# Later landing times in a planner's list of steps: an attention and MLP kernel whose order is computed at build time

## The chip, the cores and the metric

The kernel runs on one core of one Trainium2 chip. The metric is the device time of one execution in microseconds (us). Before the change it is 307.97 us, the median of three runs (307.48 to 308.44).

## The reference

Clustered attention, then an MLP. For 4 batches, 8 heads, 768 rows and 64 dimensions per head:

```
mask   = argmax(q_n . c_n) == argmax(k_n . c_n)      # 16 centroids per head, normalised rows
scores = where(mask, q k^T / sqrt(64), -1e9)
attn   = softmax(scores) ; o = attn v
x      = o as [3072 rows, 512]
h      = x @ w_in [512, 2048] ; g = h * sigmoid(h) ; out = g @ w_out [2048, 512]
```

Every row of q and k is assigned to one of 16 clusters; only pairs in the same cluster attend to each other.

## The kernel before, in words

**Parts.** The rows of q and k of a pair of heads come in by DMA (`nk`, `nq`, `nv`). A *part* prepares some of them: a scaled f16 copy `hi` (L527 to L531) and the remainder `lo` (the split, DVE, L535) go to `hl`; the rows are transposed into `ab`, in batch 0 on TensorE (L570), in batches 1 to 3 by a DMA transpose on SP's queue (`turn_dma`, L550). In batches 1 to 3 there are 24 parts, one for each batch and head, each of 12 tiles of 128x128 (6 of k, 6 of q).

**Codes.** The mask is computed inside the score matmul. On the transposed rows TensorE makes the *logits* against the centroids (L624, 12 matmuls). DVE reduces them (L641) and takes the maximum (L661), POOL subtracts it (L673), DVE marks the assigned cluster (the one-hot rows `oh`, L700 and L702) and turns them in blocks of 32 (the flip, `ohT`, L715). Four *code copies* then put `ohT` into 16 more rows of `ab` (`put`): three on POOL (L732), one as a 12 KB DMA on SP (L728). A score matmul (L801) contracts over these 80 rows, so that pairs of different clusters get a large negative score.

**Attention.** Per head 9 units of up to 512 columns: scores (L801) into a PSUM bank, exponential on ACT (L808) into `P`, then the product with v (L829, with a column for the sum), and DVE normalises (L842, L847) into `xn`. A pair of heads is turned into `xt`, by a DMA transpose on SP (`turn_x`, L866) or by TensorE (L877) and a copy on DVE or ACT (L884).

**MLP.** Batch 0 has three units of 256 rows, batches 1 to 3 two of 384 rows each. Per unit 16 *up* steps (L907, four matmuls), tanh on ACT (L913) into `tn`, the gate on DVE (L918) into `gq`, then the *down* matmuls (L942), a copy out (L955, L957) and the store (L960). The weights come in twelve pieces by POOL's DMA queue (`weight`, L974 to L980), each started after some exponential.

**What sets the order.** The program creates all steps with an engine, an estimated duration, a priority (`key`) and what they depend on. `Plan.order()` then plays them through once: at each turn it takes the step that can start first by its estimates (then the one with the lowest key), and the resulting list is emitted. Each engine executes its instructions in that order, and waits where an operand isn't there. The plan's clock is used for nothing else: it holds no time on the chip. A step's estimated end decides when its readers count as ready, and so what is put ahead of them:

```
complete(s, t + s.w + s.lag)                                   # a step on an engine
tail = self.TURNED if s.flip else self.EARLY if s.start < 2000 else self.LAND
complete(s, stop + tail + s.slack)                             # a transfer, stop: its bytes are through
```

`TURNED` is 1000 ns, `LAND` 1250. A transposing transfer enters the model's queue 300 ns after its issue, with a load of 195 ns for each tile. Buffers rotate in pools (`hl` 3, `ab` 5, `ohT` 3, `tn` 3, PSUM 8 banks), and a step takes the buffer that comes free first by the plan. TensorE also gets matmuls on zeros (L353) in gaps of the plan early on.

Of the kernel before, what the change touches and what calls it, by code (L numbers as in the profile page):

```python
# [198 lines left out]
def kernel(  # L199
# [84 lines left out]
    step = plan.step  # L284
# [17 lines left out]
    COLD = 8500.0  # L302
    MORE = 250.0
    LATE = 600
    AT = [32.0, 63.0, 104.0, 133.9, 193.2, 273.6]
    ML = [55.5, 127.6, 75.5, 138.3, 182.4, 254.3, 222.5, 316.0, 335.3, 350.3]
    PUTB = ["POOL", "POOL", "SP", "POOL"]
# [166 lines left out]
    def part(b, p, segs, a0, due, lead=20.0, hi_eng="POOL", turn="DMA", twin=False, sub="POOL", code_eng=None, pace=None, wait=None):  # L474

        key = due - lead
        span = lead / 20.0
        n = sum(j1 - j0 for _, _, j0, j1 in segs)
        if (b, p) not in abuf:
            abuf[b, p] = buf("ab")  # L480
        A = abuf[b, p]
        hl = buf("hl")
        nk, nq = nks.get((b, p)), nqs.get((b, p))
        his, los = [], []
# [18 lines left out]
        for kind, h, j0, j1, t, hs in merged:  # L503
# [35 lines left out]
            w = {"ACT": act_w(64 * m), "DVE": dve_w(64 * m, 0.55), "POOL": pool_w(64 * m)}[hi_eng]  # L539
            x = step(hi_eng, w, hi, after=lds, use=[nat, hl], key=key, pace=pace)  # L540
# [5 lines left out]
        if turn == "DMA":  # L546

            def turn_dma():
                src = T["hl"][hl.i][:, 0 : n * pitch]
                nc.sync.dma_start_transpose(T["ab"][A.i][:, a0 : a0 + n, :], src)  # L550

            turned = [step("SP", 120 * n, turn_dma, after=[his, los], use=[hl, A], key=key + 2 * span, load=195 * n, flip=True, slack=LATE)]
        else:

            Z = buf("lt")
            chunks, where = [], {}
            for hh in sorted({h for _, h, _, _, _ in runs}):
                c = [t + i for _, h, j0, j1, t in runs if h == hh for i in range(j1 - j0)]
                if chunks and len(chunks[-1]) + len(c) <= 8:
                    chunks[-1] += c  # L560
                else:
                    chunks.append(c)
            for t in sum(chunks, []):
                where[t] = len(where)

            def turn_of(c, bank, c0, c1):
                def turn_pe():
                    pt = banks[bank.i].bitcast(f16)
                    for i, t in enumerate(c):
                        nc.tensor.transpose(  # L570
                            pt[0 : c1 - c0, i * 128 : (i + 1) * 128], tiles_of(hl)[:, t, c0:c1], ident
                        )

                return turn_pe

            def settle_of(c, bank, rows_, dst, eng):
                def settle():
                    pt = banks[bank.i].bitcast(f16)[0:rows_, 0 : len(c) * 128]
                    out_ = dst()[0:rows_, where[c[0]] : where[c[0]] + len(c), :].rearrange("p n c -> p (n c)")
                    if rows_ < 128 and eng == "ACT":  # L580
                        nc.scalar.activation(out=out_, in_=pt, func=AF.Copy, bias=0.0, scale=gain[0:rows_])
                    elif rows_ < 128:
                        nc.vector.tensor_scalar(out=out_, in0=pt, scalar1=gain[0:rows_], scalar2=None, op0=ALU.mult)  # L583
                    elif eng == "ACT":
                        nc.scalar.copy(out_, pt)
                    else:
                        nc.vector.tensor_copy(out_, pt)

                return settle

            def settle_w(c, eng):
                return act_w(128 * len(c)) + 60 if eng == "ACT" else dve_w(128 * len(c), 0.55, 40)

            turned = []
            for c in chunks:
                bank = buf("M")
                x = step("PE", 57 * len(c), turn_of(c, bank, 0, 128), after=[s_ident, his, los], use=[hl, bank], key=key + 2 * span)
                turned.append(
                    step(
                        turn[0], settle_w(c, turn[0]), settle_of(c, bank, 128, lambda: T["lt"][Z.i], turn[0]),  # L600
                        after=[x], use=[bank, Z], key=key + 3 * span,
                    )
                )
# [109 lines left out]
        if turn == "DMA":  # L713
            def flip():
                nc.vector.transpose(  # L715
                    T["ohT"][ohT.i][:, 0:n, :].rearrange("p n c -> p (n c)"),
                    T["oh"][oh.i][:, 0:n, :].rearrange("p n c -> p (n c)"),
                )

            s_flip = step("DVE", dve_w(32 * n, 1.04, 95), flip, after=marks, use=[oh, ohT], key=key + 12 * span)  # L720
            placed = []
            for g in range(4):

                def put(g=g):
                    dst = T["ab"][A.i][64 : 64 + HC, a0 : a0 + n, 32 * g : 32 * g + 32]
                    src = T["ohT"][ohT.i][32 * g : 32 * g + HC, 0:n, :]
                    if code_eng[g] == "SP":
                        nc.sync.dma_start(dst, src)  # L728
                    elif code_eng[g] == "ACT":
                        nc.scalar.copy(dst, src)  # L730
                    elif code_eng[g] == "POOL":
                        nc.gpsimd.tensor_copy(dst, src)  # L732
                    else:
                        nc.vector.tensor_copy(dst, src)

                w = {"ACT": 200 + act_w(32 * n) * 0.75, "POOL": pool_w(32 * n), "DVE": dve_w(32 * n, 0.08, 240), "SP": 600}[code_eng[g]]
                load = 10 * n if code_eng[g] == "SP" else None
                placed.append(step(code_eng[g], w, put, after=[s_flip, s_log], use=[ohT, A], key=key + 13 * span, load=load, port=code_eng[g] == "DVE"))

        else:  # L740
            last = {}
            for c in chunks:
                bank = buf("M")
                x = step("PE", 57 * len(c), turn_of(c, bank, D, HW), after=[marks, his, s_ident], use=[hl, bank], key=key + 12 * span)
                x = step(
                    turn[1], settle_w(c, turn[1]),
                    settle_of(c, bank, HW - D, lambda: T["ab"][A.i][:, a0 : a0 + n, :], turn[1]),
                    after=[x], use=[bank, A], key=key + 13 * span,
                )
                for t in c:  # L750
                    last[t] = x
# [10 lines left out]
    def attention(b, h, j0, j1, key, per, turn):  # L762

        p = h // 2
        A = abuf[b, p]
        nq = j1 - j0
# [91 lines left out]
        done = xn_done[b, p, j0]  # L858
# [4 lines left out]
        if turn == "DMA":  # L863

            def turn_x():
                nc.sync.dma_start_transpose(  # L866
                    T["xt"][X.i][:, p, cols].rearrange("p (n c) -> p n c", c=128),
                    T["xn"][xn.i][:, 0:nq, :].rearrange("p n c -> p (n c)"),
                )

            x = step("SP", 1240, turn_x, after=done, use=[xn, X], key=key + per - 3, load=195 * nq, flip=True, slack=LATE)
        else:
            bank = buf("M")

            def turn_x():
                for n in range(nq):
                    nc.tensor.transpose(banks[bank.i].bitcast(f16)[:, 128 * n : 128 * n + 128], T["xn"][xn.i][:, n, :], ident)  # L877

            def settle_x():
                dst, src = T["xt"][X.i][:, p, cols], banks[bank.i].bitcast(f16)[:, 0 : 128 * nq]  # L880
                if turn == "ACT":
                    nc.scalar.copy(dst, src)
                else:
                    nc.vector.tensor_copy(dst, src)  # L884

            x = step("PE", 57 * nq, turn_x, after=done, use=[xn, bank], key=key + per - 3)
            w = act_w(128 * nq) if turn == "ACT" else dve_w(128 * nq, 0.55, 40)
            x = step(turn, w, settle_x, after=[x], use=[bank, X], key=key + per - 3)
# [80 lines left out]
    def weight(kind, n, event):  # L969

        x, use, name = event

        def f():
            nc.gpsimd.tensor_copy(pace, T[name][use.i][:, D : D + 1])  # L974
            if kind == "in":
                nc.gpsimd.dma_start(
                    win_s[:, :, ts(n, 512)], moe_w_in.rearrange("(r p) f -> p r f", p=128)[:, :, ts(n, 512)]
                )
            else:
                nc.gpsimd.dma_start(  # L980
                    wout_s[:, 2 * n : 2 * n + 2, :],
                    moe_w_out[256 * n : 256 * n + 256, :].rearrange("(c p) d -> p c d", p=128),
                )

        return step("POOL", 840, f, after=[x], use=[use], key=-1, load=2450 if kind == "in" else 1220)


    want = {(n, h): AT[n] + (AT[n + 1] - AT[n]) * h / H for n in range(NU + B - 1) for h in range(H)}
# [104 lines left out]
```

## Time and profile before

| | |
|---|---|
| median of the runs | 307.97 us (307.48 to 308.44) |
| the profiled execution | 307.14 us, of it span 305.3 us |
| TensorE clock granted (mean) | 0.998 |
| exponentials L808 on ACT | 157.8 us busy, x288 |
| scores L801 on TensorE | 90.9 us, x384 |
| up L907, down L942 on TensorE | 95.6 us x576, 97.1 us x400 |
| DMA, share of the 16 engines from 51 to 205 us | 0.80 |
| DMA, the same from 205 us to the end | 0.13 |

How to read it: busy time is the sum of the records of an engine; on TensorE (PE) the records of successive matmuls overlap, and their ends are modelled. A row of the timeline has the start in us, the length in us, the engine, the line, the operation with output<-inputs, and in brackets the idle time before it with what ended it. SPq is SP's DMA queue: a row there is the time in which SP issued a transfer, not its flight.

### The profile page before, as it was taken

Reading aid. Unit: us, or ns where it says so; the run is one execution under the profiler, and the core shown is the slowest. Engines: PE = TensorE matmul, PEld = TensorE weight load, DVE = VectorE, ACT = ScalarE, POOL = GpSimd, SP = SyncE. Lnnn points to the kernel's source line nnn. Section 1 sums busy time; section 2 is a strip of 40 time slices with the busy share of each in tenths; the row PEclk is TensorE's granted clock in tenths of the full one; section 3 lists DMA queues with packets and bytes.
Section 4 is the critical chain, followed back from the end, with each engine's and each line's share of the span. In section 5 each row is a group of like instructions: output and inputs, shape, how many; then the busy total and the mean of one; then the engine's idle time right before and its main releaser. Section 6 shows DMA issues by size and latency. Waiting matters only on the chain.

```text
span 305.3 us, 8425 instructions
## 1 busy us (share of the span) xinstructions
PE 297.3 (97%) x3257; PEld 196.1 (64%) x3257; DVE 207.9 (68%) x493; ACT 223.7 (73%) x461; POOL 108.2 (35%) x218
## 2 busy tenths in 40 slices
PE   8999999999999999999999998999999999999995
PEld 6898777577677746666656765665655565554644
DVE  5999688778869955989766997867562323750820
ACT  5869999888988838999777998778782380642721
POOL 2546432656466480717564563733000000000000
PEclk9999999999999999999999999999999999999999
DMA  7999969993969888486969848472010201002001
GB/s 245 290 249 251 206 104 224 103 248 87 226 100 237 191 167 196 138 156 162 237 149 223 155 154 169 131 129 66 0 37 36 84 12 71 35 0 73 32 34 69
DMA packets 73688, 41.82 MB, mean 137 GB/s; under 512 B 53041, under 2 KB 70705, under 8 KB 73649
## 3 DMA queue, kind: packets, MB, share of 16 engines
q1 hardware_dynamic: 68944, 36.94, 51.4%
q0 software_dynamic: 4288, 4.20, 8.6%
q8 instruction: 25, 0.41, 0.6%
q10 hardware_dynamic: 416, 0.16, 0.2%
q14 instruction: 15, 0.11, 0.1%
HBM read 27.30 MB, written 6.29 MB: 110 GB/s over the span
## 4 chain that ended last, share of the span: by engine, by line
PE 80%; DMA 7%; ACT 5%; DVE 3%; issue 1%; POOL 1%; SPq 0%; ACTq 0%; POOLq 0%
PE bank L942 27%; PE bank L907 22%; PE bank L801 16%; PE bank L829 9%; ACT P L808 4%; DMA ab<-hl 3%; PE bank L570 3%; DMA wout_s<-in_moe_w_out_dram 2%; PE bank L624 2%; DMA nk<-in_k_dram 2%; POOL hl L531 1%; PE bank L615 1%; DVE hl L535 1%; DVE gq L918 1%; PE bank L619 1%
## 5 line engine op out<-in xcount | busy, mean ns | idle before, releaser
L808 ACT ACTIVATE P<-bank 128x512 f16<-128x512 f32 x288 | 157.8, 640 | 30.8 <-PE bank L801 29.1
L942 PE MATMUL bank<-wout_s,gq 128*128 128x512 f16 (+1 forms) x400 | 97.1, 370 | 0.4 <-DMA wout_s<-in_moe_w_out_dram 0.4
L907 PE MATMUL bank<-xt,win_s 128*128 128x384 f16 (+1 forms) x576 | 95.6, 308 | 0.0
L918 DVE SCALAR_TENSOR_TENSOR gq<-tn,bank 128x384 f16<-128x384 f32 (+1 forms) x144 | 70.1, 504 | 32.4 <-ACT tn L913 28.7
L801 PE MATMUL bank<-ab 80*128 80x256 f16 (+1 forms) x384 | 90.9, 326 | 0.0
L913 ACT ACTIVATE tn<-bank 128x384 f32<-128x384 f32 (+1 forms) x144 | 67.8, 488 | 24.1 <-PE bank L907 20.9
L907 PEld LDWEIGHTS <-win_s 128*128 128x128 f16 x576 | 55.0, 97 | 28.8
L942 PEld LDWEIGHTS <-gq 128*128 128x128 f16 x400 | 37.9, 98 | 33.1 <-issue 0.7
L829 PEld LDWEIGHTS <-P 128*128 128x128 f16 x1152 | 45.6, 97 | 11.9 <-ACT P L808 0.8
L829 PE MATMUL bank<-vt,P 128*128 128x65 f16 x1152 | 49.8, 193 | 0.7 <-ACT P L808 0.6
L732 POOL COPY ab<-ohT 16x384 f16<-16x384 f16 x72 | 39.3, 546 | 28.2 <-DVE ohT L715 11.7
L801 PEld LDWEIGHTS <-ab 80*128 80x128 f16 x384 | 34.6, 97 | 20.7 <-DVE ab L583 0.2
L673 POOL TENSOR_TENSOR Df<-L,mx 128x192 f32<-128x192 f32 x24 | 12.3, 511 | 41.9 <-DVE mx L661 39.7
L957 DVE COPY ot<-bank 128x512 f32<-128x512 f32 x18 | 12.3, 681 | 16.4 <-PE bank L942 15.6
L535 DVE SCALAR_TENSOR_TENSOR hl<-nk,hl 128x384 f16<-128x384 f32 (+1 forms) x29 | 19.8, 687 | 3.3 <-POOL hl L531 3.1
L535 DVE SCALAR_TENSOR_TENSOR hl<-nq,hl 128x384 f16<-128x384 f32 (+3 forms) x33 | 20.9, 635 | 0.6 <-POOL hl L531 0.3
L641 DVE TENSOR_REDUCE L<-bank 128x192 f32<-128x384 f32 x24 | 13.3, 552 | 10.0 <-PE bank L624 9.7
L847 DVE TENSOR_TENSOR xn<-bank,rz 128x384 f16<-128x384 f32 (+2 forms) x40 | 19.1, 477 | 1.4 <-DVE rz L842 0.2
L531 POOL TENSOR_SCALAR hl<-nk 128x384 f16<-128x384 f32 (+1 forms) x25 | 13.6, 547 | 7.6 <-PE bank L570 6.7
L955 ACT COPY ot<-bank 128x512 f32<-128x512 f32 (+1 forms) x7 | 3.7, 524 | 17.2 <-PE bank L942 17.2
L531 POOL TENSOR_SCALAR hl<-nq 128x384 f16<-128x384 f32 (+2 forms) x27 | 15.2, 566 | 1.7 <-DMA nq<-in_q_dram 1.1
L417 POOL CAST vt<-nv 128x384 f16<-128x384 f32 x26 | 14.6, 582 | 1.1 <-DMA nv<-in_v_dram 0.7
(60 smaller groups left out, 183.6 us busy)
## 6 DMA issues: line engine op xcount, KB each, us to landing
nv<-in_v_dram SPq DMA_DIRECT2D x16, 384.0 KB, 5.6
out_dram<-ot SPq DMA_DIRECT2D x23, 256.0 KB, 2.3
nk<-in_k_dram SPq DMA_DIRECT2D x15, 384.0 KB, 4.3
nq<-in_q_dram SPq DMA_DIRECT2D x12, 384.0 KB, 4.7
wout_s<-in_moe_w_out_dram POOLq DMA_DIRECT2D x8, 256.0 KB, 7.2
win_s<-in_moe_w_in_dram POOLq DMA_DIRECT2D x4, 512.0 KB, 9.3
nq<-in_q_dram SPq DMA_DIRECT2D x4, 256.0 KB, 6.5
nk<-in_k_dram SPq DMA_DIRECT2D x2, 192.0 KB, 2.8
```

Source lines behind the costliest of these rows:

```text
L417: (nc.gpsimd if eng == "POOL" else nc.vector).tensor_copy(dst, src)
L531: nc.gpsimd.tensor_scalar(out=dh, in0=src, scalar1=qs, scalar2=1.0, op0=ALU.mult, op1=ALU.mult)
L535: nc.vector.scalar_tensor_tensor(out=dl, in0=src, scalar=qs, in1=dh, op0=ALU.mult, op1=ALU.subtract)
L732: nc.gpsimd.tensor_copy(dst, src)
L801: nc.tensor.matmul(banks[sb.i][:, at : at + 128 * (c1 - c0)], ab[0:80, kt[j], :], ab[0:80, qt + c0 : qt + c1, :].rearrange("p n c -> p (n ...
L808: nc.scalar.activation(out=T["P"][P.i][:, 0:at], in_=banks[sb.i][:, 0:at], func=AF.Exp, bias=0.0, scale=ESC if b else -ESC)
L829: nc.tensor.matmul(banks[O.i][:, (D + 1) * t : (D + 1) * t + nn], w, vt[:, VW * j : VW * j + nn], start=(j == 0), stop=(j == NJ - 1), skip ...
L847: nc.vector.tensor_tensor(out=T["xn"][xn.i][:, 0:nq, (h % 2) * D : (h % 2) * D + D], in0=banks[O.i][:, 0 : (D + 1) * nq].rearrange("p (t c ...
L907: nc.tensor.matmul(banks[bank.i][:, 0:n], win_s[:, r, ts(fb, 128)], T["xt"][xtb[b].i][:, r, 128 * j0 : 128 * j1], start=(r == 0), stop=(r ...
L913: nc.scalar.activation(out=T["tn"][tn.i][:, 0:n], in_=banks[bank.i][:, 0:n], func=AF.Tanh, bias=0.0, scale=1.0)
L918: nc.vector.scalar_tensor_tensor(out=T["gq"][g.i][:, fb % 4, 0:n], in0=T["tn"][tn.i][:, 0:n], scalar=1.0, in1=banks[bank.i][:, 0:n], op0=A ...
L942: nc.tensor.matmul(banks[bank.i][:, 0 : c1 - c0], T["gq"][gqs[fc // 4].i][:, fc % 4, ts(t, 128)], wout_s[:, fc, c0:c1], start=(fc == 0), s ...
```

## The change

Three allowances in the planner's model are changed. A transposing transfer (the parts of batches 1 to 3 and the `xn` of a pair of heads) counts as landed 1500 ns instead of 600 ns after the modelled end; the code copies of batches 1 to 3 on POOL count as done 600 ns later (on SP the argument has no effect, since a transfer's end doesn't use `lag`); a weight piece counts as landed 600 ns later. No instruction is added or removed, and no size changes: only the order of the list, and with it which of the rotating buffers and banks each step gets.

```diff
     LATE = 600
+    FLIP = 1500
+    DONE = 600
+    WSL = 600
...
-            turned = [step("SP", 120 * n, turn_dma, after=[his, los], use=[hl, A], key=key + 2 * span, load=195 * n, flip=True, slack=LATE)]
+            turned = [step("SP", 120 * n, turn_dma, after=[his, los], use=[hl, A], key=key + 2 * span, load=195 * n, flip=True, slack=FLIP)]
...
-                placed.append(step(code_eng[g], w, put, after=[s_flip, s_log], use=[ohT, A], key=key + 13 * span, load=load, port=code_eng[g] == "DVE"))
+                placed.append(step(code_eng[g], w, put, after=[s_flip, s_log], use=[ohT, A], key=key + 13 * span, load=load, port=code_eng[g] == "DVE", lag=Plan.LAG.get(code_eng[g], 0) + DONE))
...
-            x = step("SP", 1240, turn_x, after=done, use=[xn, X], key=key + per - 3, load=195 * nq, flip=True, slack=LATE)
+            x = step("SP", 1240, turn_x, after=done, use=[xn, X], key=key + per - 3, load=195 * nq, flip=True, slack=FLIP)
...
-        return step("POOL", 840, f, after=[x], use=[use], key=-1, load=2450 if kind == "in" else 1220)
+        return step("POOL", 840, f, after=[x], use=[use], key=-1, load=2450 if kind == "in" else 1220, slack=WSL)
```

In the list as built, TensorE's rows are the same up to the logits of the first part of batch 1 (51.6 us in the trace of before); POOL's and SP's lists differ from about there on too. From then to the last parts the logits of most parts stand behind more work than before, and some code transfers and transposes change places on SP. After the last part's logits TensorE's order is again nearly the same.

## The prediction

> **What bounds the kernel now.** The page comes first: the span, the share of TensorE (PE), and the chain that ended last.
>
> ```profile
> span 305.3 us, 8425 instructions
> PE 297.3 (97%) x3257; PEld 196.1 (64%) x3257; DVE 207.9 (68%) x493; ACT 223.7 (73%) x461; POOL 108.2 (35%) x218
> ...
> PE 80%; DMA 7%; ACT 5%; DVE 3%; issue 1%; POOL 1%; SPq 0%; ACTq 0%; POOLq 0%
> ```
>
> PE is the bound, and 80% of the chain is its own work. The change removes no instruction and adds none, so PE's 3257 matmuls stay; it can win or lose only in the time in which PE stands. How much is that? A matmul's record overlaps the next one's, so "97% busy" hides short stands. The tail of the kernel shows PE running without a break:
>
> ```profile
> 259.93 10.56 PE L907 MATMUL bank<-xt,win_s 128*128 128x384 f16 x64
> 270.33 10.52 PE L942 MATMUL bank<-wout_s,gq 128*128 128x512 f16 x48
> 280.69 10.56 PE L907 MATMUL bank<-xt,win_s 128*128 128x384 f16 x64
> ```
>
> The first group's record ends at 259.93 + 10.56 = 270.49, yet the next group starts at 270.33. So an unbroken PE starts its next matmul 0.16 us ahead of the end of the last record, and a stand is (start of a matmul − end of the record before it + 0.16). The spacings are 10.40 / 64 = 0.162 us for 384 columns and 10.36 / 48 = 0.216 us for 512. From these rows, too: from 260 us on nothing is left to win.
>
> Now the places where PE stands after 51 us (the two lists of steps are equal on PE up to there). The timeline of PE, five pairs of rows:
>
> ```profile
> 53.02 0.59 PE L801 MATMUL bank<-ab 80*128 80x512 f16 x2
> 54.00 0.38 PE L942 MATMUL bank<-wout_s,gq 128*128 128x512 f16 x1 [0.39 <-DMA wout_s<-in_moe_w_out_dram]
> ...
> 57.55 0.60 PE L942 MATMUL bank<-wout_s,gq 128*128 128x512 f16 x2
> 58.14 0.21 PE L624 MATMUL bank<-stk,ab 128*128 128x32 f16 x2
> ...
> 62.51 0.60 PE L801 MATMUL bank<-ab 80*128 80x512 f16 x3
> 63.24 0.21 PE L624 MATMUL bank<-stk,ab 128*128 128x32 f16 x2
> ...
> 136.04 0.65 PE L907 MATMUL bank<-xt,win_s 128*128 128x384 f16 x3
> 137.07 0.29 PE L624 MATMUL bank<-stk,ab 128*128 128x32 f16 x5 [0.38 <-DMA ab<-hl]
> ...
> 187.45 0.38 PE L801 MATMUL bank<-ab 80*128 80x512 f16 x1
> 188.77 0.47 PE L624 MATMUL bank<-stk,ab 128*128 128x32 f16 x12 [0.94 <-DMA ab<-hl]
> ```
>
> By that rule PE stands 0.55, 0.15, 0.29, 0.54 and 1.10 us. The first is for a weight piece (w_out). The other four all stand ahead of L624, the logits of a part, which read the transposed rows `ab` just moved by DMA: 2.08 us together. That is what this change can win, 0.7% of the time; shorter stands than 0.15 I leave out on both sides.
>
> **The change part by part.** I number the 24 parts of batches 1 to 3 by the order of their logits, 0 to 23, and give a step's place on PE as the sum of the spacings of all matmuls ahead of it. Places can be compared between the lists, because the durations are the same and PE hardly stands.
>
> *The transposing transfers (FLIP).* The planner took a 12-tile transfer to be usable 0.30 + 2.34 + 1.00 + 0.60 = 4.24 us after its issue; now 5.14.
>
> ```profile
> ab<-hl SPq DMA_TRANSPOSE x24, 4.1
> ab<-ohT SPq DMA_DIRECT2D x24, 12.0 KB, 2.8
> ```
>
> ```profile
> 183.53 3.60 SPq L550 DMA_TRANSPOSE ab<-hl  x2
> ```
>
> ```profile
> L550 SPq DMA_TRANSPOSE ab<-hl x24: 1294/1461/5414, 44.4 to 200.2; - x24
> ```
>
> The three fences are the DMA issues (last column: median us to landing), SP's timeline at part 20, and the transposes' rows on SP (min/median/max ns, while SP is held). Half the transfers land in 4.1 us or less, but PE waits for the slow half: part 20's was issued at 183.53 and its logits could start at 188.77, 5.24 later. A plan with 4.24 puts the logits 1 us early, and that is the 1.10 us stand. The Trainium skill's page "DMA: Bandwidth & Descriptors" speaks against the change here: its figures (a fixed cost of about 2.0 us, "Anatomy of one DMA", and 261 GB/s for a transpose, "Latency and other measured facts") give an estimate of 2.0 + 393 KB / 261 GB/s = 3.5 us for these 12 tiles. By that the old 4.24 would be ample and the time would stay at 307.97; the row of 4.1, and 5.24 where it matters, says otherwise, so the measurement decides.
>
> What each of the four stands becomes, by the places in the two lists:
> - Part 20 (1.10). Ahead of its logits the new list puts 6 attention matmuls (L829, 0.03 each, 0.18), a score (0.22) and two down matmuls (0.43): 0.82 us of work that stood right behind them. DVE's split rows ahead of the transfer keep their place, so it lands when it did: 1.10 − 0.82 = 0.28 stays.
> - Part 13 (0.54). Two 256-column scores (0.22) go ahead of the logits. On DVE a gate row moves behind the two splits that the transfer waits for:
>
> ```profile
> 130.02 0.54 DVE L918 SCALAR_TENSOR_TENSOR gq<-tn,bank 128x384 f16<-128x384 f32 x1
> 130.48 0.72 DVE L535 SCALAR_TENSOR_TENSOR hl<-nk,hl 128x384 f16<-128x384 f32 x1
> 131.12 0.55 DVE L535 SCALAR_TENSOR_TENSOR hl<-nq,hl 128x384 f16<-128x384 f32 x1
> ```
>
>   so the transfer can go 130.48 − 130.02 = 0.46 earlier. 0.22 + 0.46 exceeds 0.54: gone.
> - Part 1 (0.15). A score (0.22) and 18 attention matmuls (0.53) go ahead: gone.
> - Part 2 (0.29). Its logits come 0.96 earlier, but its transfer passes two entries of SP's queue (the first code transfer and a transpose of `xn`), which in the trace held SP from 55.57 to 58.18, and its splits pass part 0's one-hot rows on DVE. It is issued near 55 to 56 instead of 58.27. More than 0.96 is gained: gone.
>
> ```profile
> 55.57 1.02 SPq L728 DMA_DIRECT2D ab<-ohT  x1
> 56.97 1.21 SPq L866 DMA_TRANSPOSE xt<-xn  x1
> 58.27 4.34 SPq L550 DMA_TRANSPOSE ab<-hl  x2
> ```
>
> Together 2.08 − 0.28 = 1.80 won. The transposes of `xn` take the same allowance; the up matmuls that read them (unit 1 of the MLP) go from place 58.6 to 59.9.
>
> *The code copies (DONE).* POOL's copies count as done 0.60 later, so scores keep more room. From a part's logits to its first score the shortest room was 8.1 us (part 0) and is now 7.2 (part 1); part 0's chain in the trace ran from its logits to the landing of its code transfer:
>
> ```profile
> 51.63 0.45 PE L624 MATMUL bank<-stk,ab 128*128 128x32 f16 x12
> ```
>
> 55.57 + 2.8 − 51.63 = 6.7 us. It still fits by 0.5 us (part 1's own chain was longer only by the two transposes that held SP from 58.27 to 62.61 and now go sooner): cost nothing, and if that cover is gone, the overrun itself.
>
> *The weight pieces (WSL).* The last of the twelve goes in the unchanged part of POOL's list:
>
> ```profile
> 46.37 0.77 POOL L980 DMA_DIRECT2D wout_s<-in_moe_w_out_dram  x1
> ```
>
> The w_out piece with the 0.55 stand keeps its first reader at the same place (47.84): nothing won.
>
> *What is late next.* The new list puts part 3's logits (place 57.91) ahead of unit 1's up matmuls (59.95), and on DVE part 2's one-hot block and part 3's two reductions ahead of the `xt` copy for which those wait. Durations from this stretch:
>
> ```profile
> 63.81 0.56 DVE L641 TENSOR_REDUCE L<-bank 128x192 f32<-128x384 f32 x1 [0.39 <-PE bank L624]
> 64.41 0.35 DVE L661 TENSOR_REDUCE mx<-L 128x12 f32<-128x192 f32 x1
> 64.68 0.41 DVE L884 COPY xt<-bank 128x512 f16<-128x512 f16 x1
> 65.01 0.68 DVE L957 COPY ot<-bank 128x512 f32<-128x512 f32 x1
> 65.61 0.20 DVE L702 TENSOR_SCALAR oh<-Df 128x96 f16<-128x96 f32 x1
> 65.72 0.20 DVE L700 TENSOR_SCALAR oh<-Df 128x96 f16<-128x96 f32 x1
> 65.96 0.58 DVE L715 STREAM_TRANSPOSE ohT<-oh 128x384 f16<-128x384 f16 x1
> ```
>
> Part 2's logits at 55.56 let the reduction start 0.57 later (63.81 − 63.24), at 56.13. From a reduction's start to its one-hot rows the trace has 65.61 − 63.81 = 1.80, so 57.93, and the flip ends 0.93 on (65.96 + 0.58 − 65.61), at 58.86. Then the reduction (0.60 to the next row), the maximum (0.27) and the copy (0.41) end at 60.14; 0.2 for the release makes 60.35 against 59.95: a new stand of 0.40. Below, it could be 0, if one-hot rows come sooner; above, twice that, 0.8, if POOL's subtraction is late by as much again. I take 0.40, to which the rows lead.
>
> **Sum:** −2.08 + 0.28 + 0.40 = −1.40 us. Against the profiled execution (307.14 us, span 305.3 and 1.84 around it) that is 305.74; against the median of the runs shown, 307.97, it is 306.57. I take 306.6.
>
> **The rivals.** *Paid back.* The work put ahead of the logits must itself be ready. While PE stood 1.10 us, ACT and DVE caught up; without the stand, the score and the down matmuls put ahead of part 20 wait for a bank or a gate. And DVE now runs part 20 and 21's splits and part 19's one-hot rows ahead of a gate, some 0.64 + 0.11 + 0.24 + 0.58 = 1.6 us by the spacings above; the same happens at part 13. If PE pays most of one such block, about 1.0 us of the 1.40 are back: 307.6. For it: three `tn` buffers tie ACT to those gates. Against: up matmuls are about 1 us apart there, so three buffers cover 3 us.
>
> *Slower: SP's queue.* Part 0's code transfer now stands behind two transposes on SP. If these go at 55.0 and 56.5, SP is free near 58.0, and the code lands at 60.8. Its first score has place 56.83; part 1's logits have 51.78 and stood at 58.14, so with the 0.15 gone 6.2 are to be added, and it comes near 63.0. That is room of 2.2. But a transpose holds SP for 1.46 us in the middle and 5.41 at most (the row of L550; the longest stood behind two loads). If both take the longest, the code lands 7.9 later and PE stands 5.7; if one, 4.0 later and 1.8. It decides from 2.2 + 1.4 = 3.6 us of extra delay, where the stand eats the gain. Between 306.6 + 1.8 = 308.4 and 306.6 + 5.7 = 312.3; I take 309.4, near the lower end, since one long hold in 24 is what the trace shows. Against: no load is queued just ahead of them. The same order recurs at parts 17 and 19.
>
> *Nothing gained.* The transfers could slide by the same amount as their readers, if the splits wait for late PE work. For part 20 the list shows that they do not. The time would be 307.9.
>
> **How the numbers follow.** This kernel's measurement tells 0.3% (0.92 us) from no change, so faster is below 307.05 and slower above 308.89. Forecast 306.6: 0.52, its own range 305.6 to 307.0. The two cases in which it is paid back or not gained (307.6 to 307.9): 0.23. The queue (309.4): 0.25, which stands for other new waits of that size too, since the lists differ over 150 us. The range takes in the forecast with every stand gone and no new one (307.97 − 2.08 = 305.9, and about half of the 0.55 besides, 305.6), and the queue case up to its taken time: 305.6 to 309.4.
>
> **What would show it.** Right: no idle time of 0.3 us or more ahead of L624; at part 20 at most 0.3; PE's rows from 210 us on shifted by 1.4 us and otherwise equal; transfers still 4 to 5 us. Wrong: L801 waiting for `ab<-ohT` or POOL near 63 us; L907 waiting for the `xt` copy near 66 us by more than 0.8; L907 or L942 waiting for DVE's gates near 131 or 183 us; or logits that still wait because the transfers moved with them.

## The result, and the profile after

The changed kernel takes 305.12 us, the median of six runs (304.89 to 305.97), against 307.38 us for the kernel before on the same chip (six runs, 306.31 to 308.44). The ratio is 0.9929, with a 95% interval of 0.9905 to 0.9953: 0.7%, or 2.2 us, faster. The forecast was 306.6 us, and 305.12 lies 0.5 us below the range's low end of 305.6.

The page of the changed kernel (profiled execution: 305.97 us), the same three lines as in the prediction:

```profile
span 303.8 us, 8413 instructions
PE 297.6 (98%) x3257; PEld 196.6 (65%) x3257; DVE 206.6 (68%) x493; ACT 222.1 (73%) x461; POOL 110.2 (36%) x218
...
PE 82%; DMA 8%; ACT 3%; DVE 2%; POOL 2%; issue 1%; SPq 0%; POOLq 0%; ACTq 0%
```

PE's 3257 matmuls and their busy time are as before (297.3 then, 297.6 now). The 12 instructions fewer are waits for semaphores; each engine has as many working instructions as before. Only the time in which PE stands can have changed. Parts 13 and 20 on PE's timeline, which stood 0.54 and 1.10 us before (line numbers are 3 higher in the changed kernel, so L624 is now L627):

```profile
136.88 0.38 PE L804 MATMUL bank<-ab 80*128 80x256 f16 x2
137.10 0.46 PE L627 MATMUL bank<-stk,ab 128*128 128x32 f16 x12
...
187.89 0.59 PE L945 MATMUL bank<-wout_s,gq 128*128 128x512 f16 x2
188.32 0.45 PE L627 MATMUL bank<-stk,ab 128*128 128x32 f16 x12
```

137.10 and 188.32 are each 0.16 us ahead of the end of the record before (136.88 + 0.38 and 187.89 + 0.59): by the prediction's rule PE runs on without a break. The down matmuls at 187.89 are those that the new list puts ahead. What PE waits for now, in the view of the waits (us in total, times, longest):

```profile
PE bank L804 <- DVE xn L850: 0.6, 1, 0.6
PE bank L618 <- ACT lt L588: 0.3, 1, 0.3
PE bank L804 <- DMA ab<-ohT: 0.3, 1, 0.3
PE bank L945 <- DMA wout_s<-in_moe_w_out_dram: 0.2, 1, 0.2
```

No wait for `ab<-hl`, the transposed rows, is left in this view (one of 0.06 us at 124.5 us is too short for it). Two scores (L804) wait instead, once each. On PE's timeline these are the places, with rows of DVE and SP that explain them:

```profile
61.85 0.59 PE L945 MATMUL bank<-wout_s,gq 128*128 128x512 f16 x2
62.72 1.03 PE L804 MATMUL bank<-ab 80*128 80x512 f16 x5 [0.27 <-DMA ab<-ohT]
...
119.23 0.38 PE L804 MATMUL bank<-ab 80*128 80x512 f16 x1
120.26 0.38 PE L804 MATMUL bank<-ab 80*128 80x256 f16 x2 [0.65 <-DVE xn L850]
```

```profile
55.98 4.36 SPq L553 DMA_TRANSPOSE ab<-hl  x2
...
60.50 0.75 SPq L731 DMA_DIRECT2D ab<-ohT  x1
```

```profile
116.74 0.20 DVE L845 RECIPROCAL rz<-bank 128x6 f32<-128x6 f32 x1 [0.18 <-PE bank L832]
118.43 0.85 DVE L538 SCALAR_TENSOR_TENSOR hl<-nk,hl 128x384 f16<-128x384 f32 x1 [1.49 <-POOL hl L534]
119.20 0.55 DVE L538 SCALAR_TENSOR_TENSOR hl<-nq,hl 128x384 f16<-128x384 f32 x1
119.67 0.55 DVE L850 TENSOR_TENSOR xn<-bank,rz 128x384 f16<-128x384 f32 x1
```

At 62 us PE stands 0.43 us (62.72 − 62.44 + 0.16) for part 0's code transfer, which SP issues at 60.50, behind two transposes that hold it from 55.98 to 60.34. At 119 us it stands 0.81 us for a PSUM bank. The bank is freed by DVE's `xn` row, which the list now puts behind the splits of a part, and the first of these waits 1.49 us for POOL's `hi`.

**Stands, trace by trace.** Each kernel was traced three times (the kernel before: its first profile and the runs before_again and before_3; the changed kernel: its profile, after_again and after_3). The table adds up, by what stood behind them, all stands of 0.08 us or more between 51 and 206 us, each the time from one matmul's start to the next beyond the usual spacing of its kind, which is the prediction's rule while the clock is full; the last column adds the smaller ones too.

| trace | ahead of logits | ahead of scores | other | all, small ones too |
|---|---|---|---|---|
| before | 2.24 | 0 | 0.55 | 4.20 |
| before_again | 4.11 | 0 | 0 | 5.53 |
| before_3 | 2.49 | 0 | 0 | 3.85 |
| after | 0.37 | 1.38 | 0.35 | 3.47 |
| after_again | 0 | 0.43 | 0 | 1.85 |
| after_3 | 0.09 | 0.27 | 0 | 1.76 |
| mean before | 2.95 | 0 | 0.18 | 4.53 |
| mean after | 0.15 | 0.69 | 0.12 | 2.36 |

The means differ by 2.17 us, which accounts for the measured 2.2. The logits' stands lose 2.80, and 0.69 comes back ahead of scores.

### The profile page after: what moved, and what is told of

Its sections match the earlier page's. It is cut to its first block, busy times and chain, and to the rows that moved or that the text cites. A ratio compares the mean times of both kernels' runs of the same rounds, so it can differ in the third digit from the quotient of the medians.

```text
span 303.8 us, 8413 instructions
## 1 busy us (share of the span) xinstructions
PE 297.6 (98%) x3257; PEld 196.6 (65%) x3257; DVE 206.6 (68%) x493; ACT 222.1 (73%) x461; POOL 110.2 (36%) x218
## 4 chain that ended last, share of the span: by engine, by line
PE 82%; DMA 8%; ACT 3%; DVE 2%; POOL 2%; issue 1%; SPq 0%; POOLq 0%; ACTq 0%
PE bank L910 25%; PE bank L945 24%; PE bank L804 17%; PE bank L832 9%; PE bank L573 3%; DMA wout_s<-in_moe_w_out_dram 2%; DMA nq<-in_q_dram 2%; PE bank L627 2%; ACT P L811 2%; DMA ab<-hl 2%; DMA nk<-in_k_dram 2%; POOL hl L534 1%; PE bank L618 1%; DVE hl L538 1%; PE bank L622 1%
## 5 line engine op out<-in xcount | busy, mean ns | idle before, releaser
L804 PE MATMUL bank<-ab 80*128 80x256 f16 (+1 forms) x384 | 90.0, 325 | 0.9 <-DVE xn L850 0.6
L804 PEld LDWEIGHTS <-ab 80*128 80x128 f16 x384 | 34.7, 97 | 21.7 <-issue 1.7
L735 POOL COPY ab<-ohT 16x384 f16<-16x384 f16 x72 | 37.7, 524 | 27.3 <-DVE ohT L718 15.7
L676 POOL TENSOR_TENSOR Df<-L,mx 128x192 f32<-128x192 f32 x24 | 13.3, 554 | 28.7 <-DVE mx L664 22.2
L538 DVE SCALAR_TENSOR_TENSOR hl<-nq,hl 128x384 f16<-128x384 f32 (+3 forms) x33 | 21.7, 661 | 2.6 <-POOL hl L534 2.4
L420 POOL CAST vt<-nv 128x384 f16<-128x384 f32 x26 | 16.0, 640 | 1.1 <-DMA nv<-in_v_dram 0.8
```

The costliest lines, as they stand in the source:

```text
L420: (nc.gpsimd if eng == "POOL" else nc.vector).tensor_copy(dst, src)
L538: nc.vector.scalar_tensor_tensor(out=dl, in0=src, scalar=qs, in1=dh, op0=ALU.mult, op1=ALU.subtract)
L804: nc.tensor.matmul(banks[sb.i][:, at : at + 128 * (c1 - c0)], ab[0:80, kt[j], :], ab[0:80, qt + c0 : qt + c1, :].rearrange("p n c -> p (n ...
```

## Experiments

**The theory:** PE reads transposed rows too early in the list of before; the longer allowance puts other work ahead of the logits, and the stands go. **The rivals:** another of the edited allowances (xn's transposes, code copies, weight pieces) brings the gain; or the list is merely another one, and the difference is how two lists happen to fall; or it is enough to move the logits on PE, whatever the other engines do. How far a step moved is again told in places on PE: in the changed list the logits of the 24 parts come 1.47 us later on average (−1.65 to +5.53).

### How well the two kernels can be told apart

No edit: each kernel once more.

> The kernel before, unchanged, for a second trace. Theory A (the gain is the stands of TensorE ahead of the logits L624, which wait for a transposing transfer): the five stands at parts 1, 2, 8, 13 and 20 come back in this trace too, 2.0 to 2.4 us together, and the time is within 0.3% of before. Rival B (the stands of one trace are chance, the gain lies elsewhere): they appear at other places or are under 1 us together.

> The changed kernel, unchanged, for a second trace. Theory A: under 0.5 us of stands ahead of L624; the two stands that are new in its first trace (0.43 us ahead of L801 for a code transfer at 62 us, 0.81 us ahead of L801 for a PSUM bank at 119 us) return if the order makes them. Ratio to before 0.990 to 0.995. Rival C (the first 51 us, where the lists are equal, are what differs by chance): the ratio is within 0.3% of 1.

> The kernel before, for a third trace. The stands of 0.08 us or more ahead of the logits, between 51 and 206 us, were 2.24 and 4.11 us in the first two. Theory A (the forecast's term was read from a low trace): 3 to 4 us here too. If the first trace is the usual one: about 2.2.

> The changed kernel, for a third trace. Stands ahead of the logits were 0.37 and 0.00 us, ahead of scores 1.38 and 0.43. Theory A: under 0.4 and 0.4 to 1.4 again; the 0.43 for part 0's code transfer returns, the 0.81 at 119 us may or may not.

Measured: before_again 308.35 us, ratio to before 1.0026 (0.9995 to 1.0056); after_again 305.74 us, 0.9946 (0.9920 to 0.9972). One execution each: before_3 307.39, after_3 304.75. PE's timeline of before_again, at parts 5 and 20:

```profile
78.77 0.59 PE L942 MATMUL bank<-wout_s,gq 128*128 128x512 f16 x2
80.64 0.46 PE L624 MATMUL bank<-stk,ab 128*128 128x32 f16 x12 [1.27 <-DMA ab<-hl]
...
188.06 0.38 PE L801 MATMUL bank<-ab 80*128 80x512 f16 x1
189.75 0.47 PE L624 MATMUL bank<-stk,ab 128*128 128x32 f16 x12 [1.31 <-DMA ab<-hl]
```

Part 5 stands 1.27 + 0.16 = 1.43 us here; in the first trace of before it didn't stand at all. Part 20 stands 1.47, 1.10 and (before_3) 1.61 us. So the gain is there again, and one trace shows only some of the places that can stand. Both sums were expected otherwise: 2.0 to 2.4 us for before_again (4.11 came), 3 to 4 for before_3 (2.49 came). In after_again only part 0's score is left:

```profile
62.88 0.59 PE L945 MATMUL bank<-wout_s,gq 128*128 128x512 f16 x2
63.74 0.70 PE L804 MATMUL bank<-ab 80*128 80x512 f16 x3 [0.27 <-DMA ab<-ohT]
```

63.74 − 63.47 + 0.16 = 0.43 us, as in the first trace; the 0.81 at 119 us did not come back, here or in after_3.

### Which of the edits does it

```diff
-    FLIP = 1500      # for the parts' transposes and for those of xn
+    FLIP = 1500      # for the parts' transposes alone (xn: 600)
-    DONE = 600
-    WSL = 600
+    DONE = 0
+    WSL = 0
```

> Only the allowance of the parts' transposing transfers is 1500 ns; that of the xn transposes, the code copies and the weight pieces is as before. Each of those three alone leaves the emitted program unchanged to the last instruction, so they should matter only for which xn buffer is taken: the same time as the changed kernel, ratio 0.993 to 0.995. If one of them acts through the buffers: another ratio.

Measured: 304.89 us, ratio 0.9892 (0.9861 to 0.9923), which overlaps with the change's 0.9905 to 0.9953. Its view of the waits has no row for `ab<-hl`, and one for the codes:

```profile
PE bank L805 <- DMA ab<-ohT: 0.2, 1, 0.2
```

The lists say it still more plainly. With the allowance on xn's transposes alone, with `DONE` alone, or with `WSL` alone, the emitted program is that of before, instruction for instruction. With the parts' transposes alone it is the changed program, but for the `xn` buffer taken at some steps. So the gain is that of one of the four edits, the allowance at L550.

### How much allowance

```diff
-    FLIP = 1500
+    FLIP = 0         # 1050, 1200, 1350, 1650, 2400: one kernel each
```

All other allowances are as before, as in the last experiment.

> Only the allowance of the parts' transposing transfers, 0 ns in place of 600 (1500 in the changed kernel); the other three allowances as before. The logits stand 0.64 us earlier than in before, on average. Theory A: about 0.6 us more of stand at most parts that had none to spare (some 10 of 24), ratio 1.01 to 1.02. Rival B (any other order of this kind is as good, and before was an unlucky one): ratio 0.99 to 1.00.

> Only the allowance of the parts' transposing transfers, 1050 ns, half way. Theory A: stands at part 13 (its logits do not move) stay at 0.5, those at parts 5 and 20 go (moved by 1.9 and 1.5): ratio 0.994. Rival B: anything between 0.99 and 1.01 without a relation to the stands.

> Only the allowance of the parts' transposing transfers, 1200 ns, between 1050 (0.997) and 1500 (0.993 to 0.995). Theory A: part 20 keeps 0.3 us (its logits move by 0.82), part 13 0.3 (moved by 0.22), nothing else: 0.994 to 0.996.

> Only the allowance of the parts' transposing transfers, 1350 ns. Theory A: between 1200 (0.995) and 1500 (0.989 to 0.995), with stands ahead of the logits under 0.6 us: 0.992 to 0.995. If the time has no relation to the allowance near 1500: anything from 0.985 to 1.005.

> Only the allowance of the parts' transposing transfers, 1650 ns. Theory A: no stand ahead of the logits, stands ahead of scores begin to grow (they were 5.8 us at 2400): 0.990 to 1.002. If there is more to win beyond 1500: under 0.989.

> Only the allowance of the parts' transposing transfers, 2400 ns. Logits 7 us later on average. Theory A: no stand ahead of L624 is left, as at 1500, and nothing more is won; the codes come later and scores begin to wait: ratio 0.993 to 1.005. If more allowance still wins: under 0.990.

Measured, one trace each, with the stands counted as in the table above:

| allowance, ns | ratio to before | 95% | ahead of logits | ahead of scores | other |
|---|---|---|---|---|---|
| 0 | 1.0123 | 1.0070 to 1.0175 | 6.42 | 0.99 | 2.09 |
| 600 (before_again) | 1.0026 | 0.9995 to 1.0056 | 4.11 | 0 | 0 |
| 1050 | 0.9968 | 0.9942 to 0.9995 | 0.97 | 0 | 0.58 |
| 1200 | 0.9953 | 0.9930 to 0.9977 | 0.66 | 0.12 | 0.76 |
| 1350 | 0.9956 | 0.9928 to 0.9984 | 0.18 | 0 | 0.43 |
| 1500 (only_part_transposes) | 0.9892 | 0.9861 to 0.9923 | 0 | 0.66 | 0.20 |
| 1650 | 1.0138 | 1.0105 to 1.0170 | 0.21 | 4.26 | 4.15 |
| 2400 | 1.0163 | 1.0124 to 1.0201 | 0 | 5.82 | 1.32 |

In the traces with 0 and 1650 TensorE's clock fell to half for a few us (the last section), and the matmuls that were slow for that are in their rows. Without them the three columns are 6.24, 0.42 and 0.33 for 0, and 0, 4.08 and 2.20 for 1650. The waits of the kernel with 0:

```profile
PE bank L628 <- DMA ab<-hl: 5.3, 6, 2.1
```

Up to 1500 the stands ahead of the logits fall with every step of the allowance (600 has 2.24 and 2.49 in its other traces), and the time falls with them, as far as the intervals tell. Where the last stands would be was not foreseen: with 1050 part 20 stands and part 13 does not, where the reverse was expected. Beyond 1500 the time rises at once by more than the whole gain, and further than the 1.002 and 1.005 that were expected at most. The logits come so late that the codes made from them are late for the scores. The largest of PE's waits in the kernel with 2400:

```profile
PE bank L805 <- DMA ab<-ohT: 2.3, 3, 1.0
```

As stands by the rule these three are 2.74 us of the 5.82. The others are short, 0.13 to 0.27 us each, and most of them end with an exponential on ACT, which frees the bank. With 1650, 2.93 us wait for code copies: 2.30 for one on SP and 0.63 for one on POOL.

That a part's rows wait less and its codes wait more is one trade, and in these lists it turns between 1500 and 1650. What a single list makes of it is not smooth: between 1050 and 1350, neighbours differ by less than their intervals, and 1500 to 1650 is 2.5%.

### Only the logits, only on PE

The order of before is kept, and the logits of the parts (then also their reductions on DVE) are put later in the list by so many ns of the plan's clock; nothing is planned anew.

```diff
+    push = 0.0                                                   # of a step
-        return sorted(self.steps + extra, key=lambda s: (s.start, s.n))
+        return sorted(self.steps + extra, key=lambda s: (s.start + s.push, s.n))
+        if turn == "DMA":
+            s_log.push = 500.0          # second kernel: 1000.0, and
+            top[0].push = 600.0         # only there: the reduction (L641)
+            x.push = 300.0              # only there: the maximum (L661)
```

> The list of before; only the logits of batches 1 to 3 are emitted 500 ns of plan time later on TensorE, the other engines' lists are the same. Theory A: of the stands 0.15 and 0.29 go, 0.54 falls to about 0.1 and 1.10 to about 0.6, so about 1.4 us are won, ratio 0.995. Rival D (the gain comes from the rows that change places on DVE, POOL and SP, not from the logits' place): nothing is won, ratio 1.000.

> The list of before; the logits of batches 1 to 3 are emitted 1000 ns of plan time later on TensorE, and the two reductions behind them 600 and 300 ns later on DVE. By their places the logits stand 0.78 us later on average (the 500 ns version moved them by only 0.26, and won nothing in time). SP, POOL and ACT keep their lists. Theory A (stands ahead of L624 are what is paid): of stands of 2.2 to 4.1 us in the two traces of before, four are shorter than 0.8 and go, the two of 1.1 to 1.5 us keep 0.3 to 0.7: 1.5 to 2.5 us won, ratio 0.992 to 0.995. Rival D (the rows that change places on the other engines win it): ratio 1.000.

Measured: 500 ns gives 308.46 us, 1.0039 (1.0008 to 1.0071), with 3.03 us of stands ahead of logits; the theory's 0.995 was missed. By place these logits move by 0.26 us on average only, and 3.03 lies between the 2.24 and 4.11 of the traces of before, so this run doesn't tell the theory from the rival. 1000 ns moves them by 0.78 and gives 310.65 us, 1.0107 (1.0067 to 1.0147), slower than both expected. The push of the reductions (L643) was too small to change anything: all 24 keep their place in DVE's list, and 15 of the maxima go back by one row. PE's waits and timeline and DVE's timeline in that kernel:

```profile
PE bank L881 <- DVE xn L851: 1.7, 3, 0.9
PE bank L624 <- DMA ab<-hl: 0.9, 1, 0.9
PE bank L946 <- DVE gq L922: 0.6, 1, 0.6
```

```profile
122.71 1.25 PE L805 MATMUL bank<-ab 80*128 80x512 f16 x6
124.86 0.34 PE L881 MATMUL bank<-ident,xn 128*128 128x128 f16 x3 [0.90 <-DVE xn L851]
```

```profile
121.01 0.56 DVE L643 TENSOR_REDUCE L<-bank 128x192 f32<-128x384 f32 x1 [1.67 <-PE bank L624]
...
124.24 0.56 DVE L851 TENSOR_TENSOR xn<-bank,rz 128x384 f16<-128x384 f32 x1
```

The logits' stands do go: one is left, 1.08 us at part 20. But DVE's queue holds the reduction (L643) where it was, and DVE stands 1.67 us until the logits are there; behind it is the `xn` row for which PE then stands. In all PE stands 3.26 us for `xn` and gate rows, and 1.04 ahead of scores. It is not enough to move the logits on PE. That DVE's rows have to move with them, as they do in a list that is planned anew, is what these rows suggest; no run moved them by hand.

### The logits pulled back in the changed list

The same sort, on the changed kernel, the other way: only the logits go back on PE, and all other steps keep the order of the changed list.

```diff
+        if turn == "DMA":
+            s_log.push = -800.0
```

> The list of the changed kernel; only the logits of batches 1 to 3 are emitted 800 ns of plan time earlier on TensorE, every other engine keeps the changed kernel's list. By their places the logits stand 0.63 us earlier on average, at part 20 0.64, at part 13 0.22 and at part 1 0.75. Theory A (stands ahead of L624): part 20's room is taken back, 0.4 to 0.7 us of stand there, 0.2 to 0.6 at parts 1, 10, 11 and 13; 1.0 to 1.5 us of the gain lost, ratio to before 0.997 to 0.999. Rival D (what wins is the earlier transfers and splits on SP and DVE, with the logits' place of no weight): as the changed kernel, 0.993 to 0.995.

Measured: 307.92 us, ratio 1.0000 (0.9971 to 1.0029). By place the logits come 0.63 us earlier on average, and the whole gain is gone. The waits of this kernel, and the costliest place on PE's timeline:

```profile
PE bank L627 <- DMA ab<-hl: 0.9, 2, 0.6
PE bank L627 <- ACT P L813: 0.9, 1, 0.9
```

```profile
122.70 0.81 PE L806 MATMUL bank<-ab 80*128 80x512 f16 x4
124.38 0.46 PE L627 MATMUL bank<-stk,ab 128*128 128x32 f16 x12 [0.87 <-ACT P L813]
```

2.68 us of stands ahead of logits are back (0.15 in the mean of the three traces of the changed kernel). So it isn't true that the changed rows of the other engines win the time whatever the logits' place. But the stands aren't those that were expected. 1.32 us of them (1.03 here and 0.29 at part 4) are for a bank, and 1.21 for the rows, at parts 10 and 22. Parts 13 and 20, the steadiest places of before, don't stand at all: their transfers, issued at the places of the changed list, land 4.1 and 3.9 us after their issue, where before they took 5.2 to 5.7. At these two parts the earlier landing alone is enough, and it comes with the rest of the changed list. No run has the late landing together with the later logits, so what the later logits alone would win there isn't shown.

### The two new stands

The 0.81 us at 119 us: the row that frees the bank goes ahead of the splits. The 0.43 us at 62 us: part 0's fourth code copy goes to POOL, and no longer behind SP's transposes. Each is one edit on the changed kernel.

```diff
-        x = step("DVE", dve_w(64 * nq), norm, after=[x, pvs], use=[O, rz, xn], key=key + per - 3)
+        x = step("DVE", dve_w(64 * nq), norm, after=[x, pvs], use=[O, rz, xn], key=-1e3)
```

```diff
-    code_eng=PUTB
+    code_eng=["POOL"] * 4 if (b, p, i) == (1, 0, 0) else PUTB
```

> The changed kernel, with the key of the normalising step lowered so that it follows its reciprocal at once on DVE (in the changed kernel two splits stand between them at part 11, and the bank that the normalising step frees is what a score waits for at 119 us). If that stand of 0.81 us is made by those two rows: it goes, and the time is 0.8 us (0.3%) below the changed kernel, ratio 0.990 to before. If the bank was late for another reason: the same time as the changed kernel, ratio 0.993.

> The changed kernel with part 0's fourth code copy on POOL in place of SP's queue, where it stands behind two transposes; both traces of the changed kernel show a stand of 0.43 us ahead of the first score of part 0 for that transfer. If the queue makes it: the stand goes, 0.2 to 0.4 us below the changed kernel, ratio 0.992 to 0.994. If POOL's extra copy (0.55 us) delays the chain as much: no difference.

Measured: norm_first 306.75 us, 0.9972 (0.9946 to 0.9997); code_0_on_pool 307.17 us, 0.9971 (0.9948 to 0.9994). Neither is the expected gain. On the same chips the changed list has 0.9946 (0.9920 to 0.9972, after_again) and 0.9892 (0.9861 to 0.9923, only_part_transposes), so the second kernel is slower than that list and the first not faster. In each one's trace its stand is gone, though the 0.81 is missing from two traces of the changed kernel as well. The edit makes the planner deal out another list over the rest: in code_0_on_pool some 200 of PE's rows change place, and 0.87 us appear ahead of part 11's logits at 124 us; in norm_first PE stands at 126.6 us ahead of the same logits, and at 187 ahead of a score. The waits of code_0_on_pool have the logits at the top again, behind the start's `zeros`:

```profile
PE bank L627 <- DMA ab<-hl: 0.7, 1, 0.7
```

No kernel here is clearly faster than the changed one; the one with the parts' transposes alone has the same list.

## Why the prediction was right and where it was wrong

**Right: what bounds the kernel, and which stands go.** PE's stands were the only thing to win. Those ahead of the logits went, and one allowance alone, that of the parts' transposes, took them away. One of the prediction's own signs of being wrong came too: a score waits for `ab<-ohT` near 63 us.

**Wrong: the size of the first term.** The prediction summed the stands ahead of the logits from one trace: 2.08 us. That step failed. Three traces give 2.24 (the same trace, with one short stand more), 4.11 and 2.49, a mean of 2.95; part 5's 1.43 in before_again is a place that the prediction did not list. The saving is 2.95 − 0.15 = 2.80 where 2.08 − 0.28 = 1.80 was forecast. Term by term, −2.08 + 0.28 + 0.40 = −1.40 was forecast, and the means of the traces give −2.95 + 0.15 + 0.69 − 0.06 = −2.17, where 0.69 is ahead of scores and 0.06 the change of the other stands. The rest of the miss is the base: 307.97 was the median of three runs, and 307.38 of six. From 307.38 the forecast's −1.40 gives 305.98, inside the range; of the 1.48 us between 306.6 and 305.12, 0.59 is the base and 0.89 is size.

**Part 20: 0.28 was to stay, nothing stays.** The 0.82 us of work put ahead are there. What failed is the step "it lands when it did". Counted in places on PE, the transfer goes about 0.25 us earlier, and from its issue it lands in 3.9 us in all three traces of the changed kernel, where it took 5.2, 5.5 and 5.7 before. Part 13 has the same: 4.0 or 4.1 against 5.2 or 5.3. So these two stands, 1.88 us of the mean of 2.95, went by more than the longer room, and that was luck: nothing in the edit aims at the landing. From issue to logits part 20 has 5.2 or 5.3 us after the change, no more than before. The other parts do have more room (a median of 5.4 to 5.6 us, 4.8 to 5.0 before), and at parts 2, 3 and 21 it covers landings of 4.4 to 6.0 us. The last section shows what stands beside the late landings. Parts 1, 2 and 13 stand no more, as forecast.

**The `xt` copy near 66 us: 0.40 forecast, hidden.** DVE's timeline and PE's in the changed kernel:

```profile
64.92 0.35 DVE L664 TENSOR_REDUCE mx<-L 128x12 f32<-128x192 f32 x1
65.19 0.41 DVE L887 COPY xt<-bank 128x512 f16<-128x512 f16 x1
```

```profile
65.19 0.81 PE L804 MATMUL bank<-ab 80*128 80x512 f16 x4
65.84 1.91 PE L910 MATMUL bank<-xt,win_s 128*128 128x256 f16 x16
```

The copy ends at 65.60 and the up matmuls start at 65.84, 0.16 us ahead of the end of the scores' record (66.00): no stand. But PE had already stood 0.43 us at 62.7. In the trace of norm_first, where that stand is missing, the up matmuls do stand for the copy, by 0.18 us: it ends at 68.33 + 0.41 = 68.74 and they start at 68.80. So the term was mis-sized, and in the changed kernel the earlier of two stands in a row hides it. 0.2 us of the forecast were for the release from DVE to PE, which no run shows: here it is 0.06, and at 120.26 us in the changed kernel 0.04.

**The rival "Slower: SP's queue" did happen, at a fifth of its price.** It is that same stand, 0.43, 0.43 and 0.27 us in the three traces, and the order of events is the rival's (two transposes, then part 0's code transfer). In the first trace the queue makes it: the two transposes held SP for 4.36 us, and the issue is at 60.50 where the rival reckoned 58.0; its room of 2.2 us takes most of that. (The price of 1.8 was for a hold of 5.41 by one of them.) In the other two the issue comes 6.47 and 6.34 us after part 0's logits, as the rival reckoned (58.0 − 51.63 = 6.37); there the code takes 3.8 us to land, where 2.8 was reckoned. With 1650 a score waits 2.14 us for a code transfer as well, but SP doesn't hold that one: DVE makes its codes until 127.00 us, and it is issued at 127.19.

**"Paid back" happened once in three traces,** as 0.81 us at 119 us, for a bank behind DVE's splits. There was no such block at parts 13 and 20, where the prediction looked for it.

**Code copies, weight pieces and xn's transposes cost nothing, and for a stronger reason than given:** alone, none of them changes an instruction's place. The w_out piece that stood 0.55 us stands 0.35, 0 and 0 in the traces after, but it stood 0 in two of the three before, so that says nothing.

**The Trainium skill's page "DMA: Bandwidth & Descriptors"** led to an estimate of 3.5 us for these transposes, with which the old allowance would be ample. Its section gives the fixed cost of 2.0 us for transfers issued by GpSimd, and these are issued by SP. The runs speak against that use of it: the median landing is 3.9 to 4.1 us, the late ones take 5.2 to 6.0, and from 0 to 1500 each larger allowance took stands away.

## What to carry to other kernels

In a list that is planned ahead, the allowance on a transfer sets the place of its readers on every engine; look for the value at which the wait for the transfer and the wait for what is made from it balance, and expect a steep edge beyond it (here between 1500 and 1650 ns). Sum stands over several traces before you price them: a transfer that lands in time in one execution lands late in the next. When a step is to move, think of the rows behind it in the other engines' queues as well: where they kept their place, the wait only changed its engine. And read the landings after a change too, for a new order moves them.

## What the runs showed of the hardware that was not expected

**The landing of one and the same transfer varies by more than a microsecond.** Part 5's transpose on SP's queue and its logits on PE, in the first trace of before and then, two fences on, in before_again, whose PE rows at part 5 are shown above:

```profile
76.03 1.45 SPq L550 DMA_TRANSPOSE ab<-hl  x1
```

```profile
79.65 0.59 PE L942 MATMUL bank<-wout_s,gq 128*128 128x512 f16 x2
80.11 0.47 PE L624 MATMUL bank<-stk,ab 128*128 128x32 f16 x12
```

```profile
75.17 1.44 SPq L550 DMA_TRANSPOSE ab<-hl  x1
```

The same program: in the one, the logits start 80.11 − 76.03 = 4.08 us after the issue, and PE doesn't stand; in the other 80.64 − 75.17 = 5.47 us after it, and PE stands. The transfer itself lands 4.0 and 5.4 us after its issue (4.0 in before_3). The best allowance here, 5.14 us in the plan, is nearer to the late landing than to the median of 4.1.

**The late landings have a packet of instructions beside them.** One row of the DMA queues in the first trace of before, from 186.0 to 188.7 us, while part 20's transfer is on its way (packets, MB, share of the 16 engines):

```profile
q8 instruction: 1, 0.02, 2.7%
```

It is one packet of 16 KB, on a DMA engine for 1.18 us. In the changed kernel no such packet runs beside part 20's transfer. All 18 traces, part 1 left out (its transfer stands behind two loads), hold 414 of these transfers. Of the 282 without such a packet between 1.2 us after the issue and the landing, one takes over 5.0 us to land; of the 132 with one, 54 do. That the packet delays the transfer is the obvious reading, and no run tested it: beside part 5's transfer one runs in both traces above, and only one is late.

**A stand of about 2 us can cost twice.** In the kernel with an allowance of 1650, PE's timeline, then the granted clock by stretches (us, PE busy and count, PEld, DVE, ACT, POOL, clock, DMA share, GB/s):

```profile
125.79 0.60 PE L805 MATMUL bank<-ab 80*128 80x512 f16 x3
128.52 1.01 PE L805 MATMUL bank<-ab 80*128 80x512 f16 x2 [2.14 <-DMA ab<-ohT]
...
129.69 4.00 PE L911 MATMUL bank<-xt,win_s 128*128 128x384 f16 x12
133.49 0.86 PE L833 MATMUL bank<-vt,P 128*128 128x65 f16 x12
```

```profile
124.10:127.50 3.40, 1.58 (x13) 0.69 (x11) 2.88 (x8) 3.31 (x7) 2.42 (x5) 1.00 1.08 151
127.50:134.30 6.80, 5.78 (x39) 3.18 (x40) 2.79 (x6) 2.56 (x5) 4.37 (x10) 0.50 0.50 168
134.30:150.00 15.70, 15.70 (x198) 10.74 (x195) 13.15 (x33) 14.64 (x32) 5.86 (x12) 1.00 0.62 141
```

The stand is 128.52 − 126.39 + 0.16 = 2.29 us, with shorter ones before it. The clock falls to half in the midst of it, near 127.5 us, and is full again from 134.3. Twelve up matmuls of 384 columns take (133.49 − 129.69) / 12 = 0.317 us each, against 0.162 elsewhere; these twelve alone cost 1.9 us more. All six executions of this kernel have a mean clock of 0.989 to 0.994, so it isn't one trace's accident. The kernel with 0 shows it after a stand of 1.70 + 0.16 = 1.86 us:

```profile
139.03 0.47 PE L628 MATMUL bank<-stk,ab 128*128 128x32 f16 x12 [1.70 <-DMA ab<-hl]
```

```profile
139.90:143.40 3.50, 3.50 (x25) 1.97 (x23) 2.05 (x7) 2.13 (x5) 1.51 (x3) 0.51 1.08 348
```

It falls there once more at 194.5 us, behind a stand of 2.22. The Trainium skill's page "TensorE: Matmul & The Clock Gate" (section on the HAM clock gate) has the clock fall to half after an idle window of about 3.4 us; here PE was busy for 1.58 of the 3.4 us before the fall, with no stand that long. After before_3's stand of 1.61 us, with PE busy for 1.97 of the 3.4 us up to its end, the clock stayed at 1.00. What decides between the two was not tried.
